# Attention block with gMLP on one core: loading the q and k weights in row chunks, early keep-alive products and a recorded order

## The chip, the cores and the metric

The kernel runs on one core of a Trainium2 chip. The core has a matrix engine (TensorE, in profiles PE), a vector engine (VectorE, DVE), a scalar engine for activations and copies (ScalarE, ACT), a general engine (GpSimd, POOL) and queues that start DMA transfers (SP, and ScalarE's own). They run side by side, each through its own list of instructions in order, and wait for each other by semaphores. Products are summed in PSUM, eight banks of 128 x 512 fp32, and must be copied out by ScalarE or VectorE before a bank is used again.

The metric is the device time of one execution in microseconds. The kernel before took a median of 247.72 us in three runs (247.51 to 248.19).

## The reference

One transformer layer over 2048 tokens of width 448, all in bf16: attention (A) and a gated MLP that mixes over the tokens (B), each behind a layer norm and with a residual.

```python
def _A_ref(x, wqkv, wo):             # H = 16 heads of Dh = 28, W = 8, dil = 2
    idx = pos[:, None] - off[None, :]           # a token sees itself and 7 others, 2 apart
    logits = einsum('bhsd,bhswd->bhsw', q, kg) * scale
    attn = softmax(where(mask, logits, -1e9))
    o = einsum('bhsw,bhswd->bhsd', attn, vg)
    return o.reshape(B, S, D) @ wo
def _B_ref(x, w_in, w_sp, b_sp, w_out):         # Fh = 896
    z = gelu(x @ w_in)
    z1, z2 = z[..., :Fh], layernorm(z[..., Fh:])
    g = einsum('ts,bsf->btf', w_sp, z2) + b_sp[None, :, None]
    return (z1 * g) @ w_out
h = x + _A_ref(layernorm(x), A_wqkv, A_wo)
h2 = h + _B_ref(layernorm(h), B_w_in, B_w_sp, B_b_sp, B_w_out)
```

The token mixing with `w_sp` (2048 x 2048) is the largest product.

## The kernel before

Everything is a job: a small group of instructions on one engine, with the things that it reads and writes. `Planner.job` (L220) collects jobs, `Planner.order` (L281) places them one by one on the five lists (pe, act, dve, pool, sp) by a greedy rule: on each engine the ready job with the lowest key of the list PRIO (L27), with an estimated duration for each, and for a product that needs PSUM a Ticket of one or two banks, taken from the free ones. `Sched.issue` (L133) then turns what a job reads and writes into semaphore waits. A list `ON` (L69) says which copies go to which engine where this isn't the default.

The names that come up below:

- `load` (L592) starts a DMA (L598), or a transposing DMA (L597). FIRST (L86) gives the order of the first loads, and QENG (L87) the queue of the q,k weights: the columns of each half of the heads, 224 wide, in rows of 448 bytes, the first half on ScalarE's queue and the second on SP's, four DMAs each.
- Layer norm of x, per block of 128 tokens: statistics (L694, L696) on VectorE, the inverse deviation `rs` (L688, L689) on GpSimd, normalised rows `xn` (L705) on VectorE. The first four blocks are transposed by TensorE with an identity (L735, L737), copied into `xhT` (names xe); later blocks are transposed by DMA.
- The q,k weights arrive in `wraw` and are copied into `wqk`, where each head of 28 columns is padded to 32 (`wpad` clears it, L759; the eight copies `wp` of 128 x 448 run through `move`, L583).
- `product` (L555; its matmuls have L572): 448 rows of a sum are three whole chunks of 128 rows (jobs F) and one of 64 (job H, two such at a time on two halves of the array's rows). The q,k products run over six token ranges QT (L89), 128 and 128 tokens first, then 256, then 512, and four groups of heads; each is copied out into `qkT` (names qe).
- Per attention block b (18 of them): values v and their copy `V` (ve), logits (L863), exponential (L872), mask (L878), E.V (L887), the division (L895, L898), transposition by DMA, output projection y (L572) and residual h (L831). Then the layer norm of h, with DMA transposes into `hnT`.
- z2, per token block: product (L572), in part a copy z2c first (list RAW2), gelu (L944, L947), statistics (L951), normalisation n2 (L960), which the spatial products wait for. z1, in 14 units of two 512-column sums (seven matmul times each): product (L572) and gelu (L992).
- The spatial stage: 28 sums of 128 x 512 over 16 token blocks s, each a chain of four jobs (q = 0 to 3) of four matmuls (L1025), where job q needs z2 of blocks 4q to 4q+3; then bias (L1034), gate (L1037), the output products (L1049), the residual (L1056) and the store.
- Keep-alive products on the tile `warm` (L1064) fill the waits of TensorE at the start, as long as the planner's clock is under 9 us; `warm` is cleared on VectorE (L663). An activation that loads ScalarE's function table (L680) also reads and writes a corner of `warm`.

In the order that results, the spatial products begin between the last z2 products, and four z1 units are run later, between the spatial products.

Of the kernel before, what the change touches and what calls it, by code (L numbers as in the profile page):

```python
# [5 lines left out]
S_TOK = 2048  # L6
# [13 lines left out]
SWITCH = {"FH": 0.096, "HF": 0.096, "FL": 0.1, "HL": 0.1, "LF": 0.03, "LH": 0.1}  # L20
FILL = 0.15
TLAT = 0.9
T0 = 0.8
SAME = 0.0
LOOK = {'pe': 0.0566302904059409, 'act': 0.03215135008895764, 'dve': 0.1751563102815995, 'pool': 0.3309266053180775,
        'sp': 0.4504782353654715}
PRIO = [0, 18, 16, 17, 15, 1, 3, 7, 6, 2, 4, 11, 9, 10, 5, 8, 15, 14, 12, 13, 20, 26, 29, 28, 33, 47, 35, 48, -1, 0, 17,  # L27
# [41 lines left out]
ON = {'xe0_0': 'dve', 'xe0_1': 'act', 'nd0_4': 'pool', 'nd0_5': 'pool', 'nd0_7': 'pool', 'nd0_8': 'pool', 'nd0_10':  # L69
      'pool', 'nd0_11': 'dve', 'nd0_12': 'pool', 'nd0_13': 'pool', 'nd0_14': 'pool', 'nd0_15': 'pool', 'wp0_0': 'dve',  # L70
      'wp0_1': 'act', 'wp1_0': 'act', 'wp2_0': 'act', 'wp2_1': 'dve', 'wp3_0': 'act', 'wp3_1': 'act', 'qe0_0': 'dve', 'qe1_2':
      'act', 'qe2_1': 'dve', 'qe2_3': 'act', 'qe3_1': 'act', 'qe3_3': 'act', 'qe4_0': 'act', 'qe4_1': 'dve', 'qe4_2': 'act',
      'qe4_3': 'dve', 'qe5_0': 'act', 'qe5_3': 'act', 'od0': 'pool', 'od1': 'dve', 'od2': 'pool', 'nd1_0': 'pool', 'nd1_1':
      'pool', 'od3': 'pool', 've4': 'act', 'od4': 'dve', 'nd1_2': 'dve', 'nd1_3': 'pool', 'od5': 'pool', 'od6': 'dve',
      'nd1_4': 'dve', 'nd1_5': 'pool', 've8': 'act', 'od8': 'pool', 'nd1_6': 'pool', 'nd1_7': 'pool', 'od9': 'pool', 've10':
      'act', 'od10': 'pool', 'od11': 'pool', 'nd1_8': 'dve', 'nd1_9': 'pool', 'od12': 'pool', 'oc12': 'act', 'od13': 'dve',
      'nd1_10': 'pool', 'nd1_11': 'pool', 'od14': 'dve', 'oc14': 'act', 'od15': 'pool', 'oc15': 'act', 'nd1_12': 'dve',
      'nd1_13': 'dve', 've16': 'dve', 'oc17': 'act', 'nd1_14': 'dve', 'nd1_15': 'dve', 'z2c1': 'act', 'z2c7': 'dve', 'z2c13':
      'act'}
# [3 lines left out]
GRES = 1  # L83
WARMT = 9.0
COLD = 6.2
FIRST = [(0, 1), "q0", (1, 2), "q1", (2, 4), "v", (4, 8), (8, 12), (12, 16), "o"]  # L86
QENG = ["act", "sp"]  # L87
# [106 lines left out]
class Ticket:  # L194


    __slots__ = ("n", "b", "res")

    def __init__(self, n):
        self.n = n  # L200
        self.b = None
        self.res = Res("ticket")


class Job:
    __slots__ = ("eng", "key", "dur", "lat", "ops", "acq", "rel", "tick", "reserve",
                 "deps", "ndep", "succ", "idx", "start", "end", "name", "tbl", "srv", "kind", "alts")


class Planner:  # L210


    ENGS = ("pe", "act", "dve", "pool", "sp")
    TBL = 1.3

    def __init__(self):
        self.jobs = []
        self.filler = None

    def job(self, name, eng, key, ops, dur, lat=None, acq=None, rel=None, use=(), after=(), reserve=0, tbl=None, srv=None, kind="F", peer=None):  # L220
        j = Job()
        j.name, j.eng, j.key, j.ops, j.dur = name, eng, key, ops, dur
# [899 lines left out]
```

## Time and profile before

| what | us |
|---|---|
| median of three runs | 247.72 (247.51 to 248.19) |
| span of the profiled execution | 245.8 |
| z1 gelu, ScalarE, 14 x | 13.8 |
| exponential, ScalarE, 36 x | 31.8 |
| statistics of x and h, VectorE, 32 x | 19.1 |
| statistics of z2, VectorE, 32 x | 19.4 |
| spatial products, TensorE, 437 of 448 recorded | 101.8 |
| rs of the layer norms, GpSimd, 22 x 2 instructions | 26.3 |

A page of the profile gives the busy time of each engine, the span in 40 slices with a digit for the busy tenths, the chain of work that ended last, and groups of instructions by source line: line, engine, operation, the tile written `<-` the tiles read, the shape, how many; then busy time and mean ns of one, then the idle time of the engine ahead of them with what ended it. A row of the timeline is start, duration, engine, line, operation; a bracket behind it gives the wait ahead of it and its releaser. Matmuls overlap each other, so the mean of one is longer than the distance between two. A row of the windows is a stretch with the busy time of each engine in it. Mean durations come from the one profiled execution.

### The profile page before, as it was taken

To read this page: it belongs to the slowest core of one execution; us is meant where nothing else is said; L and a number is where in the kernel's file an instruction comes from. 1 tells how busy PE (TensorE), PEld (TensorE's weight loads), DVE (VectorE), ACT (ScalarE), POOL (GpSimd) and SP (SyncE) were. 2 spreads that over 40 slices of the span, in tenths; PEclk is the share of its full clock that TensorE was granted. 3 is DMA by queue.
4 is the path that set the end of the run, shared out by engine and by line. 5 is a ranking of instruction groups with operands and counts; after the bars stand their busy time and mean duration, and the time that the engine had idled before them with its cause. 6 is when DMAs were issued, how large, how long until landed. Compare 5 with 4: busy or idle time off the path is not lost.

```text
span 245.8 us, 4303 instructions
## 1 busy us (share of the span) xinstructions
PE 234.1 (95%) x1720; PEld 114.3 (46%) x1742; DVE 151.3 (62%) x323; ACT 96.1 (39%) x120; POOL 39.9 (16%) x96
## 2 busy tenths in 40 slices
PE   1799999999999999999999999999999999999994
PEld 1565455454545544444444444444444445444542
DVE  4498976798898989998873035314013826313823
ACT  2478869876877999852711000000000000033000
POOL 7255220034440202154211000000000000000000
PEclk9999999999999999999999999999999999999999
DMA  6945664887448598791499980000000011000102
GB/s 141 313 146 106 105 160 87 163 168 165 87 84 109 112 128 149 145 252 56 87 190 154 190 172 0 3 0 0 0 0 4 0 56 53 24 0 0 56 22 93
DMA packets 68084, 23.23 MB, mean 95 GB/s; under 512 B 61024, under 2 KB 67808, under 8 KB 68064
## 3 DMA queue, kind: packets, MB, share of 16 engines
q1 hardware_dynamic: 66976, 22.49, 44.4%
q10 hardware_dynamic: 1088, 0.46, 0.8%
q8 instruction: 14, 0.23, 0.4%
q14 instruction: 6, 0.05, 0.1%
HBM read 6.83 MB, written 1.84 MB: 35 GB/s over the span
## 4 chain that ended last, share of the span: by engine, by line
PE 87%; DVE 6%; DMA 2%; POOL 2%; issue 1%; ACTq 1%; DVEq 0%
PE psum L1025 39%; PE psum L572 33%; PE psum L1049 9%; DMA wraw<-in_A_wqkv_dram 2%; PE psum L887 2%; PE psum L863 2%; DVE st L694 1%; DVE x_tm L831 1%; POOL rs L689 1%; DVE E L878 1%; ACTq L598 1%; DVE otm L898 1%; DVE xn L705 1%; POOL rs L688 1%; DVE mv L696 0%
## 5 line engine op out<-in xcount | busy, mean ns | idle before, releaser
L992 ACT ACTIVATE z1p<-psum 128x1024 bf16<-128x1024 f32 x14 | 13.8, 1023 | 94.6 <-PE psum L572 94.6
L1025 PE MATMUL psum<-wsp_hi,z2p 128*128 128x512 bf16 x219 | 50.6, 379 | 0.3
L1034 DVE TENSOR_TENSOR ub<-psum,bb 128x512 bf16<-128x512 f32 x28 | 19.4, 692 | 50.3 <-PE psum L1025 49.5
L1025 PEld LDWEIGHTS psum<-wsp_hi,z2p 128*128 128x128 bf16 x224 | 21.8, 98 | 26.5 <-issue 0.8
L872 ACT ACTIVATE E<-psum 128x896 bf16<-128x896 f32 (+2 forms) x36 | 31.8, 928 | 4.4 <-PE psum L863 4.4
L572 PE MATMUL psum<-xhT,wqk 128*128 128x512 bf16 (+5 forms) x185 | 29.3, 323 | 0.6 <-issue 0.3
L1025 PE MATMUL psum<-wsp_lb,z2p 128*128 128x512 bf16 x109 | 25.6, 379 | 0.2
L1025 PE MATMUL psum<-wsp_la,z2p 128*128 128x512 bf16 x109 | 25.6, 379 | 0.2
L572 PE MATMUL psum<-w_in,hnT 128*128 128x448 bf16 (+1 forms) x128 | 25.0, 353 | 0.2 <-DVE otm L898 0.2
L572 PE MATMUL psum<-hnT,w_in 128*128 128x512 bf16 (+1 forms) x108 | 23.1, 379 | 0.3 <-issue 0.2
L1049 PE MATMUL psum<-w_out,z1p 128*128 128x448 bf16 (+1 forms) x119 | 22.3, 341 | 0.0
L951 DVE BATCH_NORM_STATS2 st<-z2p 128x6 f32<-128x448 bf16 x32 | 19.4, 616 | 4.2 <-ACT z2p L947 2.8
L878 DVE TENSOR_TENSOR E<-E,maskb 128x1792 bf16<-128x1792 bf16 (+2 forms) x18 | 19.6, 1104 | 1.8 <-ACT E L872 1.6
L694 DVE BATCH_NORM_STATS2 st<-x_tm 128x6 f32<-128x448 bf16 x32 | 19.1, 610 | 1.4 <-DMA x_tm<-in_A_x_dram 1.2
L572 PEld LDWEIGHTS psum<-xhT,wqk 128*128 128x128 bf16 (+1 forms) x192 | 14.3, 104 | 11.7 <-issue 2.8
L1037 DVE TENSOR_TENSOR z1p<-ub,z1p 128x512 bf16<-128x512 bf16 x28 | 11.8, 424 | 11.0 <-ACT z1p L992 10.2
L689 POOL TENSOR_TENSOR rs<-rs,negh 128x2 f32<-128x2 f32 (+2 forms) x22 | 18.1, 824 | 1.8
L688 POOL TENSOR_SCALAR rs<-mv 128x2 f32<-128x2 f32 (+2 forms) x22 | 8.2, 374 | 56.0 <-DVE mv L696 32.2
L1025 PEld LDWEIGHTS psum<-wsp_lb,z2p 128*128 128x128 bf16 x112 | 11.0, 98 | 13.2
L1025 PEld LDWEIGHTS psum<-wsp_la,z2p 128*128 128x128 bf16 x112 | 11.0, 98 | 13.1
L583 ACT ACTIVATE qkT<-psum 128x1024 bf16<-128x1024 f32 (+2 forms) x20 | 14.3, 738 | 6.4 <-PE psum L572 6.2
L1049 PEld LDWEIGHTS psum<-w_out,z1p 128*128 128x128 bf16 x119 | 11.6, 98 | 10.1
(58 smaller groups left out, 225.4 us busy)
## 6 DMA issues: line engine op xcount, KB each, us to landing
w_in<-in_B_w_in_dram SPq DMA_DIRECT2D x8, 224.0 KB, 3.2
out_dram<-srg SPq DMA_DIRECT2D x16, 112.0 KB, 1.7
x_tm<-in_A_x_dram SPq DMA_DIRECT2D x3, 448.0 KB, 6.2
w_out<-in_B_w_out_dram SPq DMA_DIRECT2D x1, 784.0 KB, 5.1
bb<-in_B_b_sp_dram SPq DMA_DIRECT2D x1, 512.0 KB, 5.3
wraw<-in_A_wqkv_dram ACTq DMA_DIRECT2D x2, 168.0 KB, 4.4
wraw<-in_A_wqkv_dram SPq DMA_DIRECT2D x2, 168.0 KB, 5.4
wv<-in_A_wqkv_dram SPq DMA_DIRECT2D x1, 336.0 KB, 5.8
```

Source lines behind the costliest of these rows:

```text
L572: ins = e.matmul(o, w, x, start=g not in seen, stop=left[g] == 0, **kw)
L583: j = pl.job(name, eng, key, [(lambda e: e.activation(o(), i(), AF.Copy) if eng == "act" else e.tensor_copy(o(), i()), list(reads), list(w ...
L689: (lambda e: e.tensor_tensor(R, A, negh[:, 0:1].to_broadcast([128, n]), ALU.pow), [rr, r_negh], r_rs[k][m:m + n])],
L694: [(lambda e: e.bn_stats(st[:, m, :], src), [rsrc], [r_st[k][m]])], dve_t(D))
L872: return e.activation(o, i, AF.Exp, scale=SCALE)
L878: return e.tensor_tensor(a, a, maskb[:, 0:1, pad:pad + nq].to_broadcast([NK, NHEAD, nq]), ALU.mult)
L951: [(lambda e, m=m, k=k: e.bn_stats(st3[:, m, k, :], z2p[:, m, D * k:D * (k + 1)]), [r_z2[m]], [r_st[2][m]])], dve_t(D))
L992: return e.activation(o, i, AF.Gelu_apprx_tanh)
L1025: ins = e.matmul(psv(tk), z2p[:, s, 128 * fc:128 * fc + 128], w[:, 512 * (tc % 2):512 * (tc % 2) + 512], start=(s == 0), stop=(s == NB - 1))
L1034: [(lambda e, tc=tc, s=s, tk=tk: e.tensor_tensor(ub[:, s, :], psv(tk), bb[:, 512 * tc:512 * tc + 512], ALU.add), [r_bb], [r_ub[s]])], dve_ ...
L1037: [(lambda e, fc=fc, tc=tc, s=s: e.tensor_tensor(z1p[:, fc, 512 * tc:512 * tc + 512], ub[:, s, :], z1p[:, fc, 512 * tc:512 * tc + 512], AL ...
L1049: ins = e.matmul(psv(tk, 0, c1 - c0), z1p[:, fc, 128 * m:128 * m + 128], w_out[:, fc, c0:c1], start=(fc == 0), stop=(fc == FC7 - 1))
```

## The change

- The q,k weights come in three DMAs of 128 whole rows (1792 bytes each) and two of 64 half rows, all on SP, and ScalarE's queue is not used. FIRST lists them behind the first x block; the recorded order (below) has the first chunk ahead of it.
- `wqk` is laid out by chunk of 128 rows, with one pad copy per chunk: three of 896 columns and one of 448, all on ScalarE, where eight of 448 were split between ScalarE and VectorE.
- The first two token ranges of q,k run chunk by chunk over all heads: three jobs of eight matmuls and one of eight half ones, into one Ticket of two banks, copied out as 2 x 512 columns on ScalarE, where it was four products with a copy of 256 columns each.
- `warm` has a tile of its own, and the table activation works on another, so that keep-alive products wait for the memset alone. There are 21 at the very start, where there were 11 in four places.
- The planner is gone. The order of all jobs (ORDER) and the banks of the tickets (BANKS) are lists, and `ON` is new: VectorE has three V copies (it had one), four z2 copies (one), and three q,k copies of 1024 columns (two); it has no pad copy (three).
- In the recorded order all z1 units and all z2 products stand ahead of the first spatial product. VectorE normalises z2 in the order of blocks 0, 1, 5, 4, 8, 6, 7, 9, 10, 2, 11, 3, 13, 12, 14, 15. Ahead of the first product with v's weights stand the same products as before, in another order.

```diff
...
-FIRST = [(0, 1), "q0", (1, 2), "q1", (2, 4), "v", (4, 8), (8, 12), (12, 16), "o"]
-QENG = ["act", "sp"]
+FIRST = [(0, 1), "q0", "q1", "q2", "q3", (1, 2), (2, 4), "v", (4, 8), (8, 12), (12, 16), "o"]
...
     def order(self):
...
+        for t, b in zip(self.tickets, BANKS):
+            t.b = b
+        return [self.jobs[i] for i in ORDER]
...
-        (wraw, o_wr), (warm, o_warm), (OT, o_ot), (ub, o_ub), (srg, o_srg) = region(
-            [("wraw", [128, 4, 2 * D], BF16), ("warm", [128, 512], BF16)],
+        warm = sb("warm", [128, 384], BF16)
+        (wq, o_wr), (OT, o_ot), (ub, o_ub), (srg, o_srg) = region(
+            [("wq", [128, 4, 2 * D], BF16)],
...
+        def load_q(c):
+
+            if c < 3:
+                load("wq%d" % c, lambda: wq[:, c, 0:2 * D], lambda: A_wqkv[128 * c:128 * c + 128, 0:2 * D], [r_wq[c]], 0.45, (1.6, 0.75))
+            else:
+                for i in range(2):
+                    load("wq%d" % (3 + i), lambda i=i: wq[64 * i:64 * i + 64, 3, 0:D],
+                         lambda i=i: A_wqkv[384:448, D * i:D * i + D], [r_wq[3 + i]], 0.45, (1.6, 0.2))
...
-        pl.job("tbl", "act", -60, [(lambda e: e.activation(warm[0:1, 0:2], warm[0:1, 0:2], AF.Exp), [r_warm], [r_warm])], 0.2, tbl="exp")
+        pl.job("tbl", "act", -60, [(lambda e: e.activation(tbt[0:1, 0:1], negh[0:1, 0:1], AF.Exp), [r_negh], [Res("tbl")])], 0.2, tbl="exp")
...
+        for c in range(4):
+            nk = 8 if c < 3 else 4
+            move("wp%d" % c, "dve", KEY["wp"] + 0.3 * c,
+                 lambda c=c, nk=nk: wqk[:, 8 * c:8 * c + nk, :].rearrange("p k (h d) -> p (k h) d", h=4)[:, :, 0:DH],
+                 lambda c=c, nk=nk: wq[:, c, 0:112 * nk].rearrange("p (h d) -> p h d", d=DH),
+                 [r_wq[c]] if c < 3 else r_wq[3:5], [r_wp[c]], {"act": act_t(112 * nk), "dve": dve_t(112 * nk, 4)})
...
+            if n == 128:
+                tk = pl.ticket(2)
+
+                def qk_small(e, lo, hi, tk, c, start, stop, parts=None):
+                    for g in range(4):
+                        for k in range(2):
+                            p, pn, kw = (0, 128, {}) if c < 3 else (64 * k, 64, {"tile_position": (64 * k, 0)})
+                            ins = e.matmul(psv(tk, k)[:, 128 * g:128 * g + 128], wap(p, pn, c, g, k), xhT[p:p + pn, c, lo:hi],
+                                           start=start and g == 0, stop=stop, skip_group_check=True, **kw)
+                    return ins
+                prev = None
+                for c in range(3):
+                    prev = pl.job("qk%dF%d" % (t, c), "pe", key, [(lambda e, lo=lo, hi=hi, tk=tk, c=c: qk_small(e, lo, hi, tk, c, c == 0, False),
+                                                                  [r_wp[c]] + xh_res(lo, hi), [])], full_t(128, 8),
+                                  acq=tk if c == 0 else None, use=[tk], after=[prev])
...
+                for k in range(2):
+                    move("qe%d_%d" % (t, k), "act", kev, lambda lo=lo, hi=hi, k=k: qkT[:, k::2, lo:hi],
+                         lambda tk=tk, k=k: psv(tk, k).rearrange("p (g t) -> p g t", g=4), [], [r_qk[t][2 * k], r_qk[t][2 * k + 1]],
+                         evac_t(512), [tk], (tk, k, 1))
...
```

More of the change, by code (lines that the diff above doesn't have):

```diff
@@ L267, in job @@
         j.deps = deps
-        j.ndep = len(deps)
-        for d in deps:
-            d.succ.append(j)
         self.jobs.append(j)
@@ L274, in hold @@
     def hold(self, j, first):
-        if first not in j.deps:
-            j.deps.add(first)
-            j.ndep += 1
-            first.succ.append(j)
+        j.deps.add(first)
     def order(self):
-        if PRIO is not None:
-            assert len(PRIO) == len(self.jobs)
-            for j in self.jobs:
-                j.key = PRIO[j.idx]
-        free = [True] * 8
-        freed_at = [0.0] * 8
-        te = {e: T0 for e in self.ENGS}
-        table = [None]
-        pstate = ["F"]
-        landed = [0.0]
@@ L292, in order @@
-        ready = {e: [] for e in self.ENGS}
-        avail = {}
-        for j in self.jobs:
-            if j.ndep == 0:
-                ready[j.eng].append(j)
-                avail[j] = 0.0
-        pend = []
-        out = []
-        left = len(self.jobs)
-        def pick_banks(n, now):
-            best = None
-            for b in range(0, 9 - n):
-                if not all(free[b:b + n]):
-                    continue
-                t = max(freed_at[b:b + n])
-                if n == 1:
-                    lone = not free[b ^ 1]
-                    k = (max(t, now), not lone, t, b)
-                else:
-                    if b % 2:
-                        continue
-                    k = (max(t, now), 0, t, b)
-                if best is None or k < best[0]:
-                    best = (k, b, t)
-            return best
@@ L395, in order @@
-        out.sort(key=lambda j: (j.start, j.idx))
-        return out
+        for t, b in zip(self.tickets, BANKS):
+            t.b = b
+        return [self.jobs[i] for i in ORDER]
 def bass_sequential_preLN__sliding_local_dilated__mixer_gmlp__prompt_kernel(
@@ L629, in bass_sequential_preLN__sliding_local_dilated__mixer_gmlp__prompt_kernel @@
-                for k in range(2):
-                    c0 = D * k + 224 * hf
-                    load("wq%d%d" % (hf, k), lambda c0=c0: wraw[:, 0:3, c0:c0 + 224],
-                         lambda c0=c0: A_wqkv[0:384, c0:c0 + 224].rearrange("(c p) n -> p c n", p=128), [W_qk[hf][k]], 0.5, (1.6, 0.6), eng=eng)
-                for i in range(2):
-                    load("wq%d_%d" % (hf, i), lambda i=i, cols=cols: cols(wraw[64 * i:64 * i + 64, 3, :]),
-                         lambda cols=cols: cols(A_wqkv[384:448, 0:2 * D]), [W_qk[hf][2 + i]], 0.6, (1.6, 0.2), eng=eng)
-            elif what == "o":
-                load_c("wo", wo, A_wo, D, r_wo2, 1.05)
+                load_q(int(what[1]))
@@ L661, in pool @@
             return pl.job(name, "pool", key, ops, dur)
-        pl.job("wset", "dve", -60, [(lambda e: e.memset(warm[:], 1.0), [], [r_warm])], 0.3)
+        pl.job("wset", "dve", -60, [(lambda e: e.memset(warm[:], 1.0), [], [r_warm])], 0.35)
         pool("ident", -59, [
@@ L753, in xh_res @@
             return [q for rr in r_xh[lo // 128:(hi - 1) // 128 + 1] for q in rr]
-        def wap(part0, np_, c, gg):
-            return wqk[part0:part0 + np_, c, gg, :]
-        r_pad = [spot("wpad%d" % i, o_wp, 4 * 8 * 256) for i in range(8)]
-        pool("wpad", -57.5, [(lambda e: e.memset(wqk[:].rearrange("p c g (h d) -> p (c g h) d", h=4)[:, :, DH:32], 0.0), [], r_pad)], 0.4)
-        for g in range(4):
-            for k in range(2):
-                move("wp%d_%d" % (g, k), "dve", KEY["wp"] + 0.3 * g,
-                     lambda g=g, k=k: wqk[:, :, 2 * g + k, :].rearrange("p c (h d) -> p c h d", h=4)[:, :, :, 0:DH],
-                     lambda g=g, k=k: wraw[:, :, D * k + 112 * g:D * k + 112 * g + 112].rearrange("p c (h d) -> p c h d", h=4),
-                     W_qk[g // 2], [r_pad[2 * g + k]], {"act": 0.5, "dve": 0.2})
+        r_wp = [spot("wp%d" % c, o_wp, 28 * 256) for c in range(4)]
@@ new lines, in bass_sequential_preLN__sliding_local_dilated__mixer_gmlp__prompt_kernel @@
+        pool("wpad", -57.5, [(lambda e: e.memset(wqk[:].rearrange("p k (h d) -> p (k h) d", h=4)[:, :, DH:32], 0.0), [], r_wp)], 0.4)
+        for c in range(4):
[4 more added lines that the diff above has]
+                 [r_wq[c]] if c < 3 else r_wq[3:5], [r_wp[c]], {"act": act_t(112 * nk), "dve": dve_t(112 * nk, 4)})
@@ L800, in values @@
             lo, hi = k0s[0], k0s[-1] + NK
-            product("v%d" % b, key, f, W_v + xh_res(lo, hi), D, 3 * nb, tk, [o_jobs.get(b + i - NV) for i in range(nb)])
+            product("v%d" % b, key, f, r_wv + xh_res(lo, hi), D, 3 * nb, tk, [o_jobs.get(b + i - NV) for i in range(nb)])
             sl = b % NV
```

188 lines of the change are left out of this document (49 added, 139 removed), and 87 rows, old and new, of tables (BANKS, ON, ORDER, PRIO).

## The prediction

> **What bounds the kernel now.** I read the page's totals first, then the windows cut at the stages, then the timeline of the head, then the groups by form and the chain of waits.
>
> ```profile
> span 245.8 us, 4303 instructions
> PE 234.1 (95%) x1720; PEld 114.3 (46%) x1742; DVE 151.3 (62%) x323; ACT 96.1 (39%) x120; POOL 39.9 (16%) x96
> DVE  4498976798898989998873035314013826313823
> core 0: us, PE busy (x) PEld busy (x) DVE busy (x) ACT busy (x) POOL busy (x), PEclk, DMA share, GB/s
> 0.00:5.10 5.10, 0.00 (x0) 0.00 (x1) 2.82 (x7) 1.49 (x2) 3.56 (x16) 1.00 0.60 133
> 5.10:10.30 5.20, 3.79 (x20) 2.03 (x21) 1.87 (x8) 1.53 (x4) 2.36 (x8) 1.00 1.01 289
> 10.30:14.20 3.90, 3.90 (x38) 3.25 (x38) 3.13 (x9) 2.43 (x6) 0.95 (x2) 1.00 1.10 316
> 14.20:17.20 3.00, 3.00 (x58) 2.15 (x55) 3.00 (x12) 2.34 (x7) 1.79 (x4) 1.00 0.27 91
> 17.20:83.20 66.00, 65.22 (x820) 33.79 (x820) 56.83 (x118) 52.99 (x63) 18.34 (x40) 1.00 0.63 121
> 83.20:126.90 43.70, 43.32 (x253) 19.48 (x257) 40.28 (x96) 30.55 (x36) 11.98 (x26) 1.00 0.70 138
> 126.90:133.90 7.00, 7.00 (x35) 3.11 (x34) 3.12 (x7) 0.92 (x1) 0.94 (x2) 1.00 1.27 182
> 133.90:242.40 108.50, 107.92 (x516) 50.45 (x523) 39.10 (x71) 3.88 (x4) 0.00 (x0) 1.00 0.16 36
> 242.40:245.80 3.40, 0.00 (x0) 0.00 (x0) 1.17 (x4) 0.00 (x0) 0.00 (x0) 1.00 0.30 101
> ```
>
> From 17.20 to 242.40 TensorE is busy 65.22 + 43.32 + 7.00 + 107.92 = 223.46 of 225.2 us; the missing 1.7 are changes between row groups and lost records. Only the first 17 us have slack. VectorE looks easy at 62%, but the slices show that its work is in the first half: until 126.90 it has 8 or 9 tenths, after that little. From 17.20 to 126.90 it is idle 12.6 us (9.2 before 83.20, 3.4 behind it). It is the engine that can become a second bound, and the end is 3.4 us of tail that the change leaves alone. The profiled execution takes 245.8 us as span; the median of the runs is 247.72, so 1.9 us lie outside the span, and I add them at the end.
>
> **The head, step by step.** The timeline, and the group of the keep-alive products:
>
> ```profile
> 0.79 0.87 SPq L598 DMA_DIRECT2D x_tm<-in_A_x_dram  x2
> 0.80 2.71 ACTq L598 DMA_DIRECT2D wraw<-in_A_wqkv_dram  x4
> 0.97 0.48 DVE L663 MEMSET warm<- 128x512 bf16 x1 [0.97 <-PEq L1107]
> 2.91 0.63 DVE L694 BATCH_NORM_STATS2 st<-x_tm 128x6 f32<-128x448 bf16 x1 [0.92 <-DMA x_tm<-in_A_x_dram]
> 3.55 1.28 ACT L680 ACT_TABLE_LOAD   x1 [3.55 <-issue]
> 4.78 0.39 DVE L705 TENSOR_SCALAR xn<-x_tm,mv,rs 128x448 bf16<-128x448 bf16 x1
> 5.10 1.25 PE L1064 MATMUL psum<-warm 128*128 128x256 bf16 x5 [5.10 <-ACT warm L680]
> 6.14 0.53 PE L735 MATMUL psum<-ident,xn 128*128 128x128 bf16 x3
> 8.51 1.04 ACT L583 ACTIVATE wqk<-wraw 128x448 bf16<-128x448 bf16 x2 [3.47 <-DMA wraw<-in_A_wqkv_dram]
> 9.29 0.50 PE L735 MATMUL psum<-ident,xn 128*128 128x128 bf16 x3 [1.41 <-DVE xn L705]
> 10.30 3.51 PE L572 MATMUL psum<-xhT,wqk 64*128 64x128 bf16 x32
> 13.81 2.33 PE L572 MATMUL psum<-xhT,wqk 128*128 128x128 bf16 x32
> 17.20 1.31 PE L572 MATMUL psum<-wv,xhT 128*128 128x448 bf16 x6
> L1064 PE MATMUL psum<-warm 128*128 128x256 bf16 x11 | 3.1, 414 | 5.1 <-ACT warm L680 5.1
> ```
>
> Now: the keep-alive products wait until 5.10 for ScalarE's first activation, which stands behind a table load that starts at 3.55 because ScalarE's queue first issues four weight loads. The q,k weights are complete at 8.5 (ScalarE waited 3.47 for them), the first q,k product starts at 10.30, and the 32 matmuls of the first block take 3.51 us where the same 32 of the second take 2.33. The first v product starts at 17.20. The work ahead of it is the same in both kernels (64 q,k matmuls, four transposed blocks, 16 logits), so that start is my milestone.
>
> Three loads of whole rows carry 3 x 229 KB instead of eight half-column loads. One SP issue costs 0.87/2 = 0.44 us. The recorded order puts chunk 0 ahead of the first x block; at the 289 to 316 GB/s of the windows its 229 KB are 0.76 us of transfer, part of which starts while x is being issued. I put x at 3.4 instead of 2.91. Bounds: no delay (x's own issue is second, +0.44 is then hidden) and the whole 0.44 + 0.76 = 1.2. Statistics to normalised row took 4.78 + 0.39 - 2.91 = 2.26 us, so xn is there at 5.7. All q,k chunks with x are 0.92 MB, 3.1 us of transfer, landed by some 5. ScalarE issues no loads, its table load moves off the path (it can start with the queue, about 0.8), and the three big pad copies follow the chunks: 0.52 each per 448 columns (the row at 8.51), so about 1.0 for 896, over at 6.2. Then transpose (0.8 with its two halves) to 6.5, two xhT copies on ScalarE to 7.4, first q,k product at 7.5: 2.8 us earlier.
>
> The keep-alive products need only their own memset and start near 1.5. Twenty-one of them at (1.25 - 0.41)/4 = 0.21 us are 4.5 us of unbroken matmuls up to 6.0, right into the transpose; before, the row at 5.10 shows five and a gap behind. A warm array does 128 columns in 0.054 us (0.2158 per 512, below, over four), a cold one in 3.51/32 = 0.11.
>
> [...]
>
> If it is warm at 7.5, the first block's 28 matmul times (24 whole, 8 halves in pairs) are 1.5 us instead of 3.5. But the new order puts xT1, xT2 and the ScalarE evacuations between the chunks: 1.5 + 0.45 + 0.45 + 1.5 + xT3 0.45 + logits 0.4, and about 1.1 of waiting for evacuations, is 5.9 up to the v product, against 6.9 before. So v starts at 13.4: **-3.8 us**. Bounds: cold until the first block is through +1.3, x late by 1.2 instead of 0.5 +0.7, giving -1.8; waiting down to nothing -4.9. The removed ScalarE queue and the merged weight layout cost nothing else. The pad copies' cover is ScalarE's idle head; if it is gone, xhT's copies are late next, which is in the 1.8. The SP transposes (from 17.17 before) start some 3 us earlier with the rest.
>
> **The new order of the middle and the engines.** Rows of the timeline, the chain in order of time and the groups by form:
>
> ```profile
> 82.87 0.37 PE L863 MATMUL psum<-qkT 28*128 28x114 bf16 x8
> 111.70 5.34 PE L1025 MATMUL psum<-wsp_la,z2p 128*128 128x512 bf16 x23
> 132.94 0.94 DVE L960 TENSOR_SCALAR z2p<-z2p,mv,rs 128x896 bf16<-128x896 bf16 x2 [1.22 <-POOL rs L689]
> 146.53 10.74 PE psum L1025 x49
> 157.32 10.74 PE psum L1025 x49
> ...
> 213.58 2.59 PE psum L572 x12
> ...
> 220.54 2.32 PE psum L572 x10
> L960 DVE TENSOR_SCALAR z2p<-z2p,mv,rs 128x896 bf16<-128x896 bf16 x16 | 7.5, 499 | 1.8 <-POOL rs L689 1.4
> L583 DVE CAST qkT<-psum 128x1024 bf16<-128x1024 f32 x2 | 2.5, 1225 | 2.3 <-PE psum L572 2.3
> L583 DVE CAST V<-psum 128x896 bf16<-128x896 f32 x1 | 1.1, 1092 | 0.0
> L583 DVE CAST z2p<-psum 128x896 bf16<-128x896 f32 x1 | 1.1, 1081 | 0.0
> L583 DVE CAST qkT<-psum 128x256 bf16<-128x256 f32 x1 | 0.4, 425 | 0.8 <-PE psum L572 0.8
> L583 DVE COPY wqk<-wraw 128x448 bf16<-128x448 bf16 x3 | 0.7, 274 | 3.3 <-DMA wraw<-in_A_wqkv_dram 3.3
> ```
>
> Before, spatial products start at 111.7, between the last z2 products, and four z1 units are kept for 213 to 224 us: TensorE has work that needs no late z2 block while VectorE finishes (last normalisation at 132.94 + 0.94 = 133.9). After, all 14 z1 units and all z2 products stand ahead of the first spatial product, which sums blocks 0 to 3, and block 3 is the twelfth of sixteen to be normalised. TensorE's work is the same in sum; what it may have lost is cover.
>
> TensorE. 50 matmuls of 512 columns in 157.32 - 146.53 = 10.79 us are 0.2158 each, 0.189 for 448. From the first spatial product on: 448 x 0.2158 + 105 x 0.189 + 14 x 0.096 = 117.9. Of 242.4 - 17.2 = 225.2 us that leaves 107.3 between the first v and the first spatial product.
>
> VectorE. Jobs moved to it: two V casts 2.18, three z2 casts 3.24, one q,k cast of 1024 1.23; off it: one q,k cast 0.43, three pad copies 0.82. Together +5.4 (an xhT copy less and an OT copy more cancel). Up to 133.9 before: 2.82 + 1.87 + 3.13 + 3.00 + 56.83 + 40.28 + 3.12 = 111.1, of which about 1.0 are two memsets of the start, the row at 0.97 and its like, so 110.1. After: + 5.4 - 4 x 0.499 (blocks normalised behind block 3) = 113.5 until the first spatial product may start, some 8 of it done by the first v: **105.5 us of VectorE work in 107.3 us of TensorE work**. If VectorE loses the 12.6 us that it loses now, the wait is 105.5 + 12.6 - 107.3 = 10.8; if it loses under 1.8, there is none. Those are the ends.
>
> Sharper by the stretch behind the last logits (83.2 before). TensorE has 14 z1 units (98 x 0.2158 = 21.1), nine z2 units and three output projections (12 x 7 x 0.189 = 15.9), and two E.V products with the row-group changes, about 1.7 (an estimate: 32 small matmuls at the 0.023 apart of the row at 82.87 are 0.7, and 1.0 for some ten changes, of the 1.7 that TensorE misses in all): 38.7. VectorE has 40.28 + 3.12 - 2.0 and some +0.8 of small jobs that change sides: 42.2. So it is 3.5 late if it never waits, 6.9 with the 3.4 that it loses there now. The first part weighs on it too: it must do 63 us in the 68.4 ahead of those logits, 92% against 56.83/66.0 = 86% now. Before, this lateness was paid with spatial products; now nothing stands behind the last z1 unit. I take the middle of 3.5 and 6.9, **+5.3 us**. Queued behind the spatial products is everything to the end, so a microsecond there is a microsecond of span.
>
> [...]
>
> Sum: 245.8 - 3.8 + 5.3 = 247.3, plus 1.9 outside the span: **249.2**. Fewer row-group changes (88 against 93) give 5/93 of the missing 1.7, 0.1, left out.
>
> **Rivals.** A (0.42): as summed; with the wait between 4.4 and 6.5, 248.3 to 250.4.
> B (0.28), the other side: VectorE's lateness is hidden. For it: it was idle 9.2 us before the last logits, its added casts are free to fill that, and the z1 units come late enough to be cover. Against: the 42.2 against 38.7. It decides where VectorE loses under about 2 us between first v and first spatial product; then the sum is 245.8 - 3.8 + 1.9 = 243.9, to 246.9 with a wait of up to 3.
> C (0.18): VectorE loses as now, 10.8 at the utmost, or the wait is one lump and the matmuls behind it run at the 0.11 of the cold head (half rate for 3.4 us, +1.7): 250.5 to 253.5. For it: the groups' idle time is for TensorE and GpSimd handoffs (L960: 1.4 for rs), which the order does not remove.
> D (0.12): the loads do not do what they are for. x stands behind a chunk, the array is still cold: only -1.8 to -2.5 of the head, and a wait of about 2 to 3: 247 to 248.5.
>
> **How the numbers follow.** About 0.3% (0.74 us: 246.98 to 248.46) is what a measurement can tell from no change. Faster: B and a bit of D, 0.29. Same: most of D and the low edge of A, 0.13. Slower: the rest of A, and C, 0.58. A's own range is 248.3 to 250.4; the cases have both signs, so the range for 8 in 10 goes from 244.4 (most of B) to 251.8 (half of C).
>
> **What would show it.** Head: first v product at 13.4, the first block's q,k matmuls 0.054 us apart, weights' pad copies over before the first transpose. If v starts after 15, D. Middle: a gap of TensorE ahead of the first spatial product that ends on VectorE's z2 normalisation, VectorE's busy time 5 us higher, and first spatial product at 13.4 + 107.3 + 5.3 = 126. If that start is at 121 to 123, B. If the first spatial matmuls are 0.43 apart, C. The prediction is wrong as a whole if TensorE waits for something else in the spatial stage, such as a late slice of the spatial weights.

## The result and the profile after

| | median of 12 runs, us | before in the same runs, us | ratio to before (95%) |
|---|---|---|---|
| changed kernel | 249.06 (247.97 to 250.60) | 247.47 (246.25 to 248.34) | 1.0080 (1.0055 to 1.0105) |

The changed kernel is slower by 0.8%. Medians here and below are of all executions; the ratios leave out those that took over 1.5% more than the fastest of their kernel (one of e1, two of e2). Its profiled execution has a span of 247.2 us, 1.4 more than before. The totals and TensorE's row of 40 slices from its page:

```profile
span 247.2 us, 4310 instructions
PE 237.0 (96%) x1752; PEld 115.7 (47%) x1752; DVE 152.1 (62%) x325; ACT 91.7 (37%) x110; POOL 40.2 (16%) x96
PE   6799999999899899899999999999999999999995
```

The same row of the kernel before:

```profile
PE   1799999999999999999999999999999999999994
```

TensorE's slices, all nines from 12 us to the last slice before, now have an eight in three places between 60 and 105 us. Windows of the changed kernel, cut at the first q,k product, the first v product, two marks in the middle and the first spatial product:

```profile
core 0: us, PE busy (x) PEld busy (x) DVE busy (x) ACT busy (x) POOL busy (x), PEclk, DMA share, GB/s
1.30:7.83 6.53, 4.55 (x27) 3.08 (x27) 2.47 (x7) 4.26 (x7) 3.72 (x15) 1.00 0.80 230
7.83:15.00 7.17, 6.84 (x95) 5.52 (x96) 5.68 (x18) 4.34 (x7) 3.61 (x8) 0.76 1.00 285
15.00:65.00 50.00, 49.84 (x630) 25.84 (x630) 45.37 (x95) 38.36 (x47) 13.04 (x28) 1.00 0.58 120
65.00:83.00 18.00, 15.22 (x169) 7.36 (x165) 16.02 (x36) 8.95 (x11) 3.23 (x7) 1.00 0.75 106
83.00:126.38 43.38, 42.32 (x279) 18.59 (x275) 39.81 (x98) 34.64 (x40) 15.02 (x34) 1.00 0.96 159
```

The first v product starts at 15.00 (17.20 before). Between 65 and 83 TensorE stands for 2.8 of 18 us, and for 1.1 more until the first spatial product at 126.38. What it waited for, largest first (engine, line and tile `<-` releaser: us in total, times, longest), from the view of waits:

```profile
PE psum L455 <- DMA hnT<-xn: 2.4, 2, 1.3
PE psum L965 <- DVE warm L541: 1.4, 1, 1.4
PE psum L656 <- ACT xhT L466: 1.3, 1, 1.3
PE psum L613 <- DVE xn L583: 0.6, 1, 0.6
PE psum L455 <- DVE OT L466: 0.6, 1, 0.6
PE psum L926 <- DVE z2p L861: 0.4, 1, 0.4
PE psum L764 <- DVE otm L799: 0.4, 1, 0.4
PE psum L455 <- DMA wv<-in_A_wqkv_dram: 0.3, 1, 0.3
```

The four that name warm (1.4), xhT (1.3), xn (0.6) and wv (0.3) lie ahead of the first v product. Behind it the largest are not in front of the spatial products (0.4) but at two z2 products that wait for DMA transposes of the normalised h, at 68.6 and 81.5. The chain of waits of the changed kernel at these places, in order of time (start, duration, what):

```profile
63.80 4.67 DMA hnT<-xn
68.60 5.48 PE psum L455 x30
...
77.08 4.24 DMA hnT<-xn
81.46 1.30 PE psum L455 x6
...
126.38 69.37 PE psum L926 x320
```

Between 101.75 and 126.38 this chain runs through statistics and normalisations on VectorE and `rs` on GpSimd: the normalisation of z2 was just in time there, with 0.4 of waiting.

Where the 1.4 us come from, from starts and ends in the two profiles:

| stretch | before | after | difference |
|---|---|---|---|
| start to first v product | 17.20 | 15.00 | -2.2 |
| first v to the end of the last product | 242.35 - 17.20 = 225.2 | 233.80 + 10.77 - 15.00 = 229.6 | +4.4 |
| from there to the end of the span | 3.4 | 2.6 | -0.8 |

(The last group of output products in the timeline before, and below it after:)

```profile
236.68 5.67 PE L1049 MATMUL psum<-w_out,z1p 128*128 128x448 bf16 x36
```

```profile
233.80 10.77 PE L950 MATMUL psum<-w_out,z1p 128*128 128x448 bf16 x63
```

### The profile page after: what moved, and what is told of

Read it like the earlier page. It is cut to its first block, busy times and chain, and to the rows that moved or that the text cites. A ratio compares the mean times of both kernels' runs of the same rounds, so it can differ in the third digit from the quotient of the medians.

```text
span 247.2 us, 4310 instructions
## 1 busy us (share of the span) xinstructions
PE 237.0 (96%) x1752; PEld 115.7 (47%) x1752; DVE 152.1 (62%) x325; ACT 91.7 (37%) x110; POOL 40.2 (16%) x96
## 4 chain that ended last, share of the span: by engine, by line
PE 70%; DVE 12%; DMA 9%; SPq 4%; POOL 3%; issue 2%; DVEq 0%
PE psum L926 39%; PE psum L455 19%; PE psum L950 9%; DMA hnT<-xn 4%; SPq L481 3%; DVE st L852 3%; DMA OTs<-otm 3%; DMA wv<-in_A_wqkv_dram 2%; POOL rs L567 2%; PE psum L764 2%; DVE x_tm L732 2%; DVE st L572 2%; PE psum L788 2%; DVE z2p L861 1%; DVE E L779 1%
## 5 line engine op out<-in xcount | busy, mean ns | idle before, releaser
L935 DVE TENSOR_TENSOR ub<-psum,bb 128x512 bf16<-128x512 f32 x28 | 19.3, 691 | 66.5 <-PE psum L926 66.1
L455 PE MATMUL psum<-w_in,hnT 128*128 128x448 bf16 (+1 forms) x128 | 24.5, 353 | 2.4 <-DMA hnT<-xn 2.4
L455 PE MATMUL psum<-xhT,wqk 128*128 128x512 bf16 (+3 forms) x128 | 24.9, 354 | 0.2 <-ACT E L773 0.2
L455 PE MATMUL psum<-hnT,w_in 128*128 128x512 bf16 (+1 forms) x112 | 24.1, 380 | 0.0
L950 PE MATMUL psum<-w_out,z1p 128*128 128x448 bf16 (+1 forms) x119 | 21.7, 342 | 0.0
L852 DVE BATCH_NORM_STATS2 st<-z2p 128x6 f32<-128x448 bf16 x32 | 18.7, 608 | 0.3 <-ACT z2p L845 0.2
L567 POOL TENSOR_TENSOR rs<-rs,negh 128x2 f32<-128x2 f32 (+2 forms) x22 | 17.1, 778 | 1.8
L926 PEld LDWEIGHTS psum<-wsp_lb,z2p 128*128 128x128 bf16 x112 | 10.9, 98 | 13.4 <-issue 0.4
L455 PEld LDWEIGHTS psum<-w_in,hnT 128*128 128x128 bf16 (+1 forms) x128 | 10.0, 97 | 14.5 <-issue 4.1
L957 DVE TENSOR_TENSOR srg<-psum,x_tm 128x448 bf16<-128x448 f32 (+1 forms) x17 | 10.1, 597 | 8.7 <-PE psum L950 8.3
L466 ACT ACTIVATE qkT<-psum 128x1024 bf16<-128x1024 f32 (+1 forms) x16 | 13.3, 839 | 3.9 <-PE psum L455 3.8
```

The lines of the kernel that those rows point to most:

```text
L455: ins = e.matmul(o, w, x, start=g not in seen, stop=left[g] == 0, **kw)
L466: j = pl.job(name, eng, key, [(lambda e: e.activation(o(), i(), AF.Copy) if eng == "act" else e.tensor_copy(o(), i()), list(reads), list(w ...
L567: (lambda e: e.tensor_tensor(R, A, negh[:, 0:1].to_broadcast([128, n]), ALU.pow), [rr, r_negh], r_rs[k][m:m + n])],
L852: [(lambda e, m=m, k=k: e.bn_stats(st3[:, m, k, :], z2p[:, m, D * k:D * (k + 1)]), [r_z2[m]], [r_st[2][m]])], dve_t(D))
L926: ins = e.matmul(psv(tk), z2p[:, s, 128 * fc:128 * fc + 128], w[:, 512 * (tc % 2):512 * (tc % 2) + 512], start=(s == 0), stop=(s == NB - 1))
L935: [(lambda e, tc=tc, s=s, tk=tk: e.tensor_tensor(ub[:, s, :], psv(tk), bb[:, 512 * tc:512 * tc + 512], ALU.add), [r_bb], [r_ub[s]])], dve_ ...
```

## The experiments

All are the changed kernel with lists edited: which engine runs a copy (`ON`), the order on one engine (ORDER, shown here with the names of the jobs), and, where the order of products changes, the banks (BANKS) that follow from it. All compute the whole reference. Each was timed in rounds beside the kernel before. Theory 1 is the prediction's: VectorE's work is what TensorE waits for.

**e1 and e2: VectorE relieved.**

```diff
 ON
-'ve2': 'dve', 've4': 'dve', 've6': 'dve',                        (e1)
-'z2c1': 'dve', 'z2c3': 'dve', 'z2c4': 'dve', 'z2c10': 'dve'      (e1, e2)
 (without an entry these copies run on ScalarE)
```

> The changed kernel with its three V copies and four z2 copies (3 x 1.09 + 4 x 1.09 = 7.6 us of VectorE) on ScalarE, order as it is. Theory 1 (VectorE's work is what TensorE waits for between the first v product at 15.0 and the first spatial product at 126.4): the first spatial product starts at 122.3 to 123.5 (15.0 + 107.3 of TensorE work, and what remains of the waits), the time falls by 3 to 4 us, to about 245.5, below the kernel before. Theory 2 (the waits come from the order alone: transposes of h issued late on SP, no spatial products as cover): first spatial product within 1 us of 126.4 and the time within 1 us of 249.1. Theory 3 (ScalarE becomes late instead): first spatial product at 126 or later, with waits of TensorE that end on ScalarE's V or z2 copies.

> The changed kernel with its four z2 copies alone (4.3 us of VectorE, all behind 70 us) on ScalarE. Theory 1: work on VectorE counts wherever it lies ahead of 126.4, so about 4.3/7.6 of what e1 gains, some 2 us less than the changed kernel. If only the early V copies make the chain of h late: within 0.5 us of 249.1. Theory 2: within 0.5 us.

**e3 and e4: the head.** e4 has the edits of e1 and of e3.

```diff
 order on SP
-... x2 wv wq3 x4 wo wv_1 wo_1 x8 wo_0 wv_0 x12
+... x2 wv wq3 x4 wv_1 wv_0 x8 wo wo_1 wo_0 x12
 order on pe
-21 x warm, xT0, qk0F0
+26 x warm, xT0, 10 x warm, qk0F0
```

> The changed kernel with fifteen more keep-alive products (five ahead of the first transpose, ten behind it) and the two half-row loads of v's weights ahead of those of wo and of the third block of x. The granted clock stays full from 4.6 us on, the first 24 q,k matmuls take 1.4 us in place of 2.6, the first v product starts at 13.4 to 14.2 in place of 15.0. Theory 1: the first spatial product stays at 126 (125.5 to 126.6), since VectorE has no less to do, and the time stays within 0.6 us of 249.1. Rival (TensorE is the bound and each microsecond of the head counts): first spatial product and time 0.8 to 1.6 us lower.

> e1 and e3 together. Theory 1: with VectorE relieved TensorE is the bound again and the head counts: first v at 13.4 to 14.2, first spatial product 0.8 to 1.6 us ahead of e1's, time about 244.3. Theory 2: as e3. Theory 3: as e1's, no gain over e1.

Measured:

| | median, us | ratio to before (95%) | first v, us | last logits | first spatial |
|---|---|---|---|---|---|
| changed kernel | 249.06 | 1.0080 (1.0055 to 1.0105) | 15.00 | 85.3 | 126.4 |
| e1 | 247.41 | 1.0019 (0.9996 to 1.0042) | 15.16 | 85.4 | 125.2 |
| e2 | 247.95 | 1.0013 (0.9984 to 1.0042) | 15.55 | 85.8 | 126.0 |
| e3 | 246.94 | 0.9993 (0.9966 to 1.0019) | 14.22 | 84.5 | 125.2 |
| e4 | 247.25 | 1.0004 (0.9981 to 1.0026) | 14.32 | 85.1 | 125.7 |

Gains on the changed kernel are differences of two such ratios, uncertain by about 0.35% or 0.8 us. The last two columns are the start of the last logits product and of the first spatial product in the one profiled execution. e1 gains 0.6%, some 1.5 us, where theory 1 asked for 3 to 4, and its first spatial product is not at 122.3 to 123.5. e2, which moves only 4.3 of the 7.6 us, gains 0.7%, as much within the noise: near what theory 1 asked of it, so the z2 copies do count, and the V copies add nothing that can be told. What is left is told by windows of e1 and its view of waits:

```profile
65.00:83.00 18.00, 15.75 (x187) 7.97 (x183) 12.15 (x28) 11.77 (x15) 2.65 (x6) 1.00 0.78 107
...
83.00:125.20 42.20, 41.75 (x277) 18.79 (x277) 40.52 (x103) 35.40 (x40) 15.75 (x35) 1.00 0.95 167
```

```profile
PE psum L454 <- DMA hnT<-xn: 1.8, 2, 1.7
```

Between 65 and 83 VectorE is now busy 12.15 of 18 us, a third of the stretch free, and TensorE still waits there for a transpose of h. So VectorE's load alone is not what makes that transpose late. e3 gains 0.9%, some 2.2 us, where theory 1 expected nothing; in its profile the first v is 0.8 earlier and the first spatial product 1.2. It has two edits, the keep-alive products and the order of the loads, and no run tells them apart. And e4, with 0.8%, is no better than e3. Theory 1 alone falls. That the gains of e1 and e3 do not add is a hint of something behind both, no more than that with 0.8 us of uncertainty on each, and no run here shows what it is.

**e5 and e6: the order of the middle.** The changed kernel up to the first v product, and behind it the order and the engines of the kernel before; e6 with e3's head.

```diff
 order, all engines
-all jobs behind xT3 as recorded in the changed kernel
+the same jobs, as they follow in the kernel before (lg1_1 ahead of v0F)
 ON, BANKS: those of the kernel before, as far as they concern these jobs
```

> The changed kernel's loads, keep-alive products, pad copies and order up to the first v product; behind it the order and the engines of the kernel before (spatial products between the last z2 products, four z1 units late). Same computation. Theory A (the new order of the middle costs the time, the new head saves it): first v at 15.0 to 15.2, no wait of TensorE over 0.6 us behind it, time 2 us below the kernel before, about 245.2. Theory B (what runs late in the middle comes from engines that are equally loaded in both orders, so an earlier head only makes TensorE wait later): time within 0.7 us of the kernel before, with waits of 1 us and more between 60 and 110.

> e5 with the head of e3 (fifteen more keep-alive products, v's half rows loaded earlier). Theory A: another 0.8 us less than e5 (first v at 14.2), about 244.4. Theory B: as the kernel before.

e5: 247.53 us, 1.0040 of before (1.0017 to 1.0062). e6: 247.70, 1.0022 (0.9997 to 1.0048). Half of theory A holds: behind the first v product there is no wait over 0.2 us in either profile. But no time is won. The order of before runs the logits of block 1 ahead of the first v product. In e6's profile TensorE waits 1.55 for their q,k copies, in e5's 1.28 for the last `xn` and then 0.30 for these copies; in both the granted clock is lower behind it, in e6 0.68 from 14.8 to 18.2 and 0.84 from 18.2 to 22.0. Windows of e5:

```profile
9.10:12.50 3.40, 2.88 (x53) 2.10 (x54) 1.58 (x4) 2.72 (x6) 1.41 (x4) 1.00 1.05 315
12.50:15.90 3.40, 1.81 (x31) 1.11 (x30) 3.40 (x11) 3.40 (x6) 1.33 (x2) 1.00 0.56 160
15.90:19.30 3.40, 3.40 (x14) 1.63 (x14) 3.37 (x13) 0.82 (x1) 2.21 (x6) 0.50 0.17 36
```

The granted clock (PEclk) is 0.50 from 15.9 to 19.3: half of 3.4 us, 1.7, is lost to matmuls of full width that ran at 1.00 before. The record has the mean granted clock of each execution, and one such stretch lowers it to 0.993. Eight of e5's twelve executions lie at 0.993 or below, with a median of 248.08, four at 0.998 or above, with 247.00; in e6 eight at 0.993 or below have 247.82 and four at 0.999 or above 246.22. So the half clock costs 1.1 to 1.6 us, but without it e6 is only 0.5 below the kernel before (246.73) and e5 not below it: what else kept the expected 2 us away stays open.

**e7, e8, e10 and e11: SP's list.** SP issues the transposing DMAs one after another. Its timeline in the changed kernel:

```profile
59.30 1.20 SPq L480 DMA_TRANSPOSE OT<-otm  x1
60.55 1.26 SPq L480 DMA_TRANSPOSE hnT<-xn  x1
61.85 1.26 SPq L480 DMA_TRANSPOSE OT<-otm  x1
63.16 0.59 SPq L481 DMA_DIRECT2D w_in<-in_B_w_in_dram  x1
63.80 4.94 SPq L480 DMA_TRANSPOSE hnT<-xn  x3
68.78 2.57 SPq L480 DMA_TRANSPOSE OT<-otm  x2
71.39 1.27 SPq L480 DMA_TRANSPOSE OTs<-otm  x1
72.71 1.27 SPq L480 DMA_TRANSPOSE hnT<-xn  x1
74.02 1.27 SPq L480 DMA_TRANSPOSE OTs<-otm  x1
75.33 1.30 SPq L480 DMA_TRANSPOSE wsp_la<-in_B_w_sp_dram  x1
```

Each start is the end of the one ahead plus 0.05: from 59.3 to 76.6 the list has no free place (the three hnT take 1.1 more than 3 x 1.27). Among these and near them, at 54.4, 57.3, 75.3, 80.8 and 82.1, stand slices of the spatial weights (wlo), which no product reads before 126.

```diff
 order on SP
-... oT6 hT0 wlo2 w_in3_0 wlo0 w_in2_1 ... oT12 wlo3 hT7 hT6 wlo13 wlo12 oT13 ... hT15 whi4 ... whi3 wlo11 whi7 whi15
+... oT6 hT0 w_in3_0 w_in2_1 ... oT12 hT7 hT6 oT13 ... hT15 wlo2 wlo0 wlo3 wlo13 wlo12 whi4 ... whi3 wlo11 whi7 whi15        (e7, e8)
+... the same, but ... hT15 wlo2 wlo0 wlo3 wlo11 wlo13 wlo12 whi4 ... whi3 whi7 whi15                                        (e10, e11)
 e8 and e11 have the edits of e4 too
```

> The changed kernel with five transposing loads of spatial weights (6.5 us of SP's list between 55 and 83) moved behind the last transpose of h. Theory S (SP's list, one transposing DMA after another at 1.27 us, is what is late between 60 and 84): the waits of 1.2 and 1.5 at 68.6 and 81.5 shrink to under 0.5 in sum, first spatial product 1.5 to 2.5 us earlier than 126.4, time about 247. Theory 1 (VectorE): waits and time as in the changed kernel, within 0.7 us.

> e4 with the same five loads moved. Theory S: with VectorE, the head and SP relieved TensorE waits under 1 us in sum behind the first v at 14.3, first spatial product at 122 to 123, time about 244.3, 2.5 us below e4. If VectorE's chain and not SP is the floor that e1 to e4 share: within 0.7 us of e4.

> e7 with the slice of spatial weights that it made late (TensorE waited 5.5 us for it at 143) placed right behind the last transpose of h too. Theory S: as e7 up to 124 (waits at 68 and 81 gone, first spatial product at 124), no wait behind it, so 2.4 us below the changed kernel, about 246.7 against a kernel before of 247. Theory 1 (VectorE alone): first spatial product back at 126, time 249.

> e8 (VectorE, head and SP relieved) with that slice placed in the same way. Theory S and 1 together: first v at 14.3, first spatial product at 122 to 123, no wait behind it, 244 to 245; where the first v comes late again as in e8 (16.5), about 2 more. If one of the three relieves the same wait as the others: no better than e10, 246.7.

e7 took 254.92 us (1.0314 of before), e8 253.49 (1.0278): both far off what was expected, by a fault of the edit. One more slice, already behind the others on SP's list, was pushed back to where TensorE had to wait for it. From e7's view of waits:

```profile
PE psum L924 <- DMA wsp_lb<-in_B_w_sp_dram: 5.3, 1, 5.3
```

Ahead of that place e7 is as theory S has it: the first v at 14.94, the first spatial product at 123.97 in place of 126.38. e8 is not: its granted clock was 0.64 from 11.4 to 14.8 and 0.86 from 14.8 to 18.2, behind a wait of 1.5 for `xn`, its first v came at 16.56 and its first spatial product at 124.8, not at 122 to 123. e10 and e11 put that slice in its place:

| | median, us | ratio to before (95%) | first v | last logits | first spatial |
|---|---|---|---|---|---|
| e10 | 246.95 | 1.0011 (0.9990 to 1.0032) | 15.55 | 83.4 | 124.6 |
| e11 | 245.28 | 0.9939 (0.9920 to 0.9959) | 14.72 | 82.9 | 122.5 |

Windows of e10 and of e11 for the stretch that lost 2.8 us in the changed kernel:

```profile
65.00:83.00 18.00, 17.40 (x206) 8.69 (x203) 16.65 (x36) 11.18 (x15) 3.61 (x7) 1.00 0.45 75
```

```profile
65.00:83.00 18.00, 17.59 (x204) 8.92 (x200) 13.84 (x34) 13.56 (x17) 3.99 (x8) 1.00 0.40 70
```

e10 takes nothing off VectorE, which is even busier (16.65 against 16.02), and TensorE is busy 17.40 in place of 15.22. From first v to first spatial product e10 takes 109.0 us and e7 109.0, against 111.4 in the changed kernel. So these slices, where they stood, caused the two long waits, and e10 is 0.7% below the changed kernel, some 1.7 us, near the 2.4 expected. How they did it was not told apart. For the list speaks that in e7, whose first v differs by 0.06 only, the transposes ahead of the first wait start 1.1 earlier (62.67 against 63.80). Against it, ahead of the second wait the changed kernel's list was free from 76.63 to 77.08, and the transposes there waited for their rows. And the DMA share falls from 0.75 to 0.45, so the transfers themselves may have been in the way. The gain of this edit adds to that of e4: e11 is 1.4% below the changed kernel, about 3.5 us (1.7 and 1.9 alone), and faster than the kernel before by 0.6%, with no wait over 0.4 us behind the first v product. On top of e10 the edits of e1 and e3 together are worth 1.8 us, no more than without it, which gives no sign that SP's slices kept those two from adding.

**e9 and e12: the order of before, with the new head put right.**

```diff
 order on pe, against e6
-... xT3, lg1_1, v0F ...
+... xT3, v0F, lg1_1 ...                     (e9, e12)
-... qk0F2, xT1 ...
+... qk0F2, 10 x warm, xT1 ...               (e12)
```

> e6 with the first v product directly behind the fourth transpose (as in the changed kernel), ahead of the logits of block 1 that made TensorE wait 1.7 us in e6. Theory A: no wait over 0.6 us between 12 and 16, so the array stays at full clock from 11.5 us on, first v at 14.2 to 15.0, 225 us from there to the last product as in the kernel before, so 2 to 3 us below the kernel before: 244 to 245. If the middle is bound by VectorE or SP in that order too: TensorE waits of 1 us and more appear between 60 and 110 and the time is within 0.7 us of the kernel before.

> e9 with ten more keep-alive products ahead of the second transpose, where TensorE stood 1.35 us in e9 and the granted clock fell to half for the next 3.4 us. If such standing time in a stretch of 3.4 us is what closes the gate: the granted clock is full from 6 us on without a break, the first v product starts at 14.2 to 15.0 in place of 16.1, 224.9 us from there to the last product as in the kernel before, so 1.1 to 1.9 us below e9, about 244.4. If the half clock of e9 has another cause: the clock falls again between 12 and 16 and the time is within 0.5 us of e9's 245.75.

e9: 245.75 us, 0.9950 of before (0.9931 to 0.9968). e12: 246.01, 0.9971 (0.9954 to 0.9988). e9 is faster than before by 1.2 us, where theory A asked for 2 to 3. In its profile no wait behind the first v product is over 0.2, but the granted clock was 0.50 from 12.5 to 15.9 and the first v came at 16.08 only. Windows of e9, and below them of e12:

```profile
9.10:12.50 3.40, 2.05 (x32) 1.36 (x30) 2.61 (x8) 1.98 (x4) 2.28 (x6) 1.00 1.07 330
12.50:15.90 3.40, 3.40 (x46) 2.42 (x43) 3.40 (x12) 2.52 (x5) 1.33 (x2) 0.50 0.49 142
```

```profile
8.00:11.40 3.40, 3.40 (x48) 3.06 (x46) 2.59 (x9) 0.76 (x2) 2.28 (x6) 1.00 1.05 334
11.40:14.80 3.40, 3.40 (x68) 2.59 (x66) 3.40 (x12) 3.26 (x6) 1.29 (x2) 1.00 0.79 241
```

In e12's profile the clock stays at 1.00 and the first v starts at 14.85, as expected of the clock, and its span is 0.7 shorter than e9's (244.4 against 245.1). Its median is not: the intervals of e9 and e12 overlap, and the gain of 1.1 to 1.9 us did not come. The mean clocks on record give the likely reason: e9's profiled execution is the only one of its twelve with a half-clock stretch (0.992, the others 0.998 to 1.000), and at 246.85 us the longest. The expectation was read from that one; the median of e9 had nothing for e12 to mend. What keeps both from theory A's 244 to 245 stays open.

## Why the prediction came out, and where its steps were wrong

The time was forecast at 249.2 and is 249.06; the first spatial product was forecast at 126 and starts at 126.38. The sum was 245.8 - 3.8 + 5.3; it is 245.8 - 2.2 + 4.4 - 0.8. The sign was right for the reason given in general form (the head gains, and the new middle loses more), but the term of the middle was put on one engine alone. That the number fits to 0.2 us is luck: the head came 1.6 too late, the middle 0.9 and the tail 0.8 better than forecast, and these errors cancelled.

- **The head.** The steps up to the first q,k product held. Timeline of the changed kernel:

```profile
1.38 4.03 PE L965 MATMUL psum<-warm 128*128 128x256 bf16 x21 [1.38 <-DVE warm L541]
3.74 0.63 DVE L572 BATCH_NORM_STATS2 st<-x_tm 128x6 f32<-128x448 bf16 x1 [1.88 <-DMA x_tm<-in_A_x_dram]
7.83 2.59 PE L656 MATMUL psum<-xhT,wqk 128*128 128x128 bf16 x24 [1.26 <-ACT xhT L466]
15.00 1.29 PE L455 MATMUL psum<-wv,xhT 128*128 128x448 bf16 x6 [0.34 <-DMA wv<-in_A_wqkv_dram]
```

  x came at 3.74 (forecast 3.4), the first q,k product at 7.83 (7.5), inside the bounds; the second and third pad copies ended at 7.23 instead of 6.2, and the xhT copies behind them are what the q,k product waited for. Two steps failed. The 24 matmuls took 2.59 us, where 24 at the forecast 0.054 are 1.3: this is the prediction's bound for a cold array. That the 21 early products would have the array at full clock at 7.5, and with it the 1.5 us for the first block in the sum of -3.8, was the author's assumption. No run shows a head of -3.8: the earliest first v measured is e3's 14.22, 3.0 ahead of before. The same 21 products left different heads: the changed kernel's granted clock is 1.00 from 4.6 to 8.0 and 0.50 from 8.0 to 11.4, where TensorE, busy throughout, has 37 matmuls; in e5 it is 1.00 until 15.9, and 44 matmuls take 2.76 us from 8.0 to 11.4. In e11 and e12, which have more early products, the 24 took 1.50. And the last half row of v's weights landed late: the new order on SP has it sixteenth, TensorE waits 0.34 for it, and the sum had no term for it. e3 has edits for both, and its first v starts at 14.22. How much of the time the half clock costs in this kernel is open: of the changed kernel's twelve executions seven have a mean clock of 0.993 or below, with a median of 248.93, and the five at 0.999 or above are no shorter, with 249.62.
- **The middle: mis-sized and given to one engine alone.** The prediction had VectorE with 105.5 us of work against 107.3 of TensorE between first v and first spatial product, and so 3.5 to 6.9 late. TensorE's part is right: it is busy 49.84 + 15.22 + 42.32 = 107.4 in that stretch. VectorE's is not: it is busy 45.37 + 16.02 + 39.81 = 101.2, 10 us short of the 111.4 that it had. Over the whole span its busy time went up 0.8 us, from 151.3 to 152.1, not 5. The durations did grow: counts times means of its groups add up to 164.8 us before and 169.1 after, 4.3 more. But busy time counts overlapping instructions once, and the overlap of neighbours grew from 13.4 to 17.0; it is 13.0 in e9, which has the old order, so it goes with the order. The prices of the moved casts were about right: without seven of them, 7.6 us by their means, e1's busy time is 145.4, 6.7 less. What was wrong was to add them to a busy time as if the overlap stayed. In the 38.7 of TensorE behind the last logits, the 1.0 for some ten changes between row groups is an estimate that no run shows: of the 1.7 that TensorE misses before, four gaps of 0.16, 0.6 in all, stand at changes to all 128 rows (at 38.2, 56.6, 67.8 and 105.1), one of them behind the last logits.

  VectorE is still part of the stall. From first v to first spatial product the changed kernel takes 111.4 us, e1 110.0, e2 110.4, e10 109.0 and e11 107.8, near the 107.3 of work. In these single executions the slices on SP are worth about 2.4 of the 4.1 us and VectorE's copies 1.0 to 1.4. e4, with 111.3, does not fit that; why is open.
- **Where the stall goes.** It was looked for in front of the spatial products, where 0.4 us came to stand; 2.4 of it stands at two products that wait for transposes of h. That SP carries spatial slices among these transposes has no term in the sum; the prediction named only a slice that itself comes late. e10 shows this term.
- **The tail** of 3.4 us was taken as fixed and is 2.6; why was not tried.
- **The rivals.** Case C's half rate for 3.4 us behind a lump of waiting, its +1.7, was an assumption that no run shows: no such lump came in the middle, where the longest wait is 1.3, and PEclk is 1.00 in every window from 15.00 to 126.38. e5 has such a stretch, 0.50 from 15.9 to 19.3, but behind waits of 1.28 and 0.30. B fails for the changed kernel and is near what e11 is: with nothing late, the first spatial product is at 122.5, inside the 121 to 123 given as B's sign. D's cold array came as 2.59 us for the 24 matmuls, and the head's gain of 2.2 lies in D's 1.8 to 2.5; the time lies in A's range with a middle at the lower edge of A's 4.4 to 6.5.

## What to carry to other kernels

Before a wait for a DMA is put down to the engine that fed it, look at the list of the queue, and ask of each transfer in it when it is first needed: here five transfers that were not needed for more than 40 us cost 1.7 us where they stood. Single gains are not a sum: e1, e3 and e10 gain 1.5, 2.2 and 1.7 us, and all three together 3.5. When work is moved to an engine, its mean durations (4.3 us more here) are not what its busy time grows by (0.8): the overlap of neighbours can change with the order (13.4 us before, 17.0 after). And one profile is one execution: where the clock differs between executions, look at the mean clock of each before explaining a median by the profile.

## What the runs showed of the hardware

Ahead of 20 us the granted clock was 0.50 for 3.4 us in the profile of the changed kernel (8.0 to 11.4), in e5's (15.9 to 19.3) and in e9's (12.5 to 15.9). In the 3.4 us ahead of it TensorE was busy for 1.50, 1.81 and 2.05 us, 44 to 60%, and no single wait there was over 1.3 us. Windows of the changed kernel:

```profile
4.60:8.00 3.40, 1.50 (x15) 0.93 (x14) 1.33 (x3) 2.33 (x4) 1.65 (x5) 1.00 0.93 282
8.00:11.40 3.40, 3.40 (x37) 2.95 (x34) 2.49 (x8) 0.94 (x2) 2.28 (x6) 0.50 1.03 327
11.40:14.80 3.40, 3.27 (x62) 2.38 (x58) 2.82 (x10) 3.19 (x6) 1.14 (x2) 0.99 1.02 252
```

The waits in the first row are the 0.6 and 1.3 in the view above; behind the second, fully busy, the clock was 0.99. In e3, 2.46 of 3.40 (the row below) was followed by 1.00.

```profile
8.00:11.40 3.40, 2.46 (x41) 1.84 (x37) 2.61 (x8) 1.40 (x3) 2.28 (x6) 1.00 1.09 339
```

Busy time alone does not decide it. In the changed kernel 1.97 of 3.40 (65.2 to 68.6) and 2.06 (79.7 to 83.1) were followed by 3.4 us at 1.00. What else counts, these runs do not show.

PEclk also reads 1.00 where matmuls ran as slowly as at 0.50. In the kernel before it is 1.00 from 10.30 to 14.20, and yet the 32 q,k matmuls of the first block took 3.51 us; in the changed kernel the same number, most of them at 0.50, took 2.59 + 0.61, and in e11 at 1.00 they took 1.50 + 0.40. In e10 it is 1.00 from 8.0 to 11.4, and yet TensorE, busy throughout, has 40 matmuls in this row, against 48 in that of e12 above:

```profile
8.00:11.40 3.40, 3.40 (x40) 3.03 (x37) 2.33 (x7) 0.93 (x2) 2.27 (x6) 1.00 1.01 310
```

So a head with slow matmuls need not show in PEclk, nor in the mean clock of an execution: the profile of before has a mean of 1.000.
